# Attention, an expert layer and a tanh layer in one kernel: a rare branch made shorter, its count moved ahead, and a conversion step moved to GpSimd

## The chip, the core and the metric

One NeuronCore of a Trainium2 chip runs the whole program. The metric is the device time of one execution in microseconds, smaller is better. Before the change the median of 3 runs is 900.23 us (898.01 to 905.54). PE is TensorE, DVE VectorE, ACT ScalarE, POOL GpSimd, and SP the engine that issues most DMA transfers.

## What is computed

Three layers follow each other, all in float32, with two batches of 768 tokens.

```python
mask = q_bucket[:, :, :, None] == k_bucket[:, :, None, :]        # 6-bit sign hash of q and k
scores = np.where(mask, scale * np.matmul(q, k.transpose(0, 1, 3, 2)), -1e9)
x = softmax(scores) @ v                                          # 16 heads, then (1536, 512)
noisy = x @ w_gate + np.log1p(np.exp(x @ w_noise)) * noise       # 8 experts, the best 2 per token
out[mask] += top2_w[mask, k, None] * (np.maximum(x[mask] @ w1[e], 0) @ w2[e])
h = x @ w_in                                                     # 512 to 2048
return (h - np.tanh(h)) @ w_out                                  # 2048 to 512
```

The last layer's weights arrive as float64, and the kernel turns them into float32 itself.

## The kernel before, in words

**Precision.** A float32 product is made of three PE products: every operand is split into a high part that PE takes as it is and a low remainder, and high times high, high times low and low times high are summed. ACT makes the high part of a weight (L999), DVE or POOL the low one (L998). The same holds for activations (L1217, L1218 for inputs, L1288, L1290 for the hidden layer).

**Attention** comes first, in frames that a plan lays out; the change does not touch it.

**Experts.** Tokens are put into rows of their experts by indirect DMA. The nine segments `segs` are computed in turn: n = 0 and n = 1 are the two halves of expert 0's tokens (first batch, second batch), n = 2 to 8 the experts 1 to 7, each in eight steps f over 128 hidden columns. A step is 12 matmuls up (`h_mm`/`h_arm`, L1257) and, per block of tokens, 3 matmuls down (`y_mm`, L1297 to L1299). Segments from n = 1 on choose how many columns to multiply by the count of tokens: `ARMS` lists the widths, `pick_arm` branches on PE, `load_arm` reads the choice into a PE register. The inputs of the next segment are loaded by `load_x` and transposed by `trans_x` (L1216) during the current one.

**Segment 0 and the gate.** `seg_fine(0)` cuts segment 0 into 32 pieces (16 half steps up of 6 matmuls, 16 down products of 3 matmuls), and `fill(n, keep)` issues n of them unless only `keep` are left. They lie between the small steps of the second batch's gate (`gate(B-1)`), which DVE works off one after the other. At the end of this gate stand, in this order: the row indices for the scatter (`pick`), two low parts of weights that were held back (`lows`, L998), the totals of all experts (`totals`, L909 to L920), the arms, and the largest excess of an expert over its capacity (`excess`, L922 to L932), whose last instruction writes the count `cmi` (L931). `KEEP` pieces are left for after the branch, and `TX` says at how many remaining pieces each of segment 1's four transpositions is issued.

**The branch.** `overflow()` reads `cmi` on every engine (L1464) and enters a body only if an expert has more tokens than its 448 rows (L1465); with these inputs it is jumped over. The body is a slow, complete recomputation: a loop over experts, a loop over blocks of 128 tokens, and inside that eight hidden steps written out one after the other. Behind the branch come some warm-up products (`warm(WARM[4])`, L1649, L202), transpositions of segment 1, the kept pieces and the first step of segment 1.

**Weights and conversions.** In the loop over segments each step f may issue, on SP: `load_x`, `store()` (results of the segment before, and converted weights to the DRAM tile `W2f`, L1079), and then `fetch()` (raw weights of a coming step, L1027 to L1031). From (n, f) = (2, 3) to the end of n = 7, `convert_more` works off the float64 weights, 16 tiles of 128x1024: ACT takes the absolute value, and six DVE steps follow (L1068, L1070, L1072, L1074, L1076, L1078). The tiles `cv_g`, `cv_p`, `cv_a` and `cv_w` have one buffer each; L1076 writes `cv_w` first, L1078 adds into it, and a DMA carries it to `W2f`. Two steps are done per f, three in every odd f of n = 2 and n = 7. POOL makes low parts of weights in n = 1 and n = 7, and in n = 3 and 4 it issues nine indirect DMAs that sort an index table (`order`, L972); otherwise it has nothing to do from n = 2 to n = 6.

**Order.** PE, DVE, ACT, POOL and SP each work off their instructions in the order in which they are written, and wait for each other by semaphores.

Of the kernel before, what the change touches and what calls it, by code (L numbers as in the profile page):

```python
# [6 lines left out]
F32 = mybir.dt.float32  # L7
# [5 lines left out]
U32 = mybir.dt.uint32  # L13
# [8 lines left out]
PF = 3  # L22

FILL = (2, 0, 3, 1, 3, 1, 0, 0, 4, 2, 0, 0)
FILL2 = 2
TX = (2, 2, 0, 0)
BANKS = {'a': [0, 1, 7], 'b': [2, 3], 'c': [4, 5], 'd': [6]}

PLAN = dict(turn=(-23, -15, -19, -10), turn1=(-20, -18, -13, -10), sign=(-12, -7), sign2=5, sign1=(-9, -7), gap=0,
# [16 lines left out]

JOIN = (4, 5, 5)

WARM = (7, 1, 2, 10, 3)

POOL1 = 7

# [1 line left out]

CVN = 2

KEEP = 2

FA = 4

# [4 lines left out]

POOL_W = 4

ARMS = {0: ((96, 0), (104, 0), (112, 0), (128, 0)),
        1: ((124, 0), (128, 0), (128, 16), (128, 64))}
LN2 = 0.6931471805599453  # L70
NEGB = -8.0e9
# [17 lines left out]
def body(tc, q, k, v, proj, w_gate, w_noise, noise, w1, w2, w_in, w_out, out):  # L89
# [25 lines left out]
    with ExitStack() as ctx:  # L115
# [20 lines left out]
        def bank(tag):  # L136
            r = banks[tag]
            nbank[tag] += 1
            n = r[nbank[tag] % len(r)]
            if n in held:  # L140
                return held[n]
            return psp.tile([128, 512], F32, tag=f"b{n}", name=f"bank{n}")
# [523 lines left out]
        def gate(b):  # L666
# [120 lines left out]
            if early:  # L787
# [3 lines left out]
                eng.tensor_copy(basev[:, 1, 0:1], late0)  # L791
                eng.tensor_scalar(late0, late0, float(1 - FIRST), None, op0=ALU.add)
            yield
            ts = w("g_ts", [128, NC, E])
            if early:
                eng.tensor_scalar(ts, over, BIG, None, op0=ALU.mult)
# [123 lines left out]
            pick_arms(0, 0, 1)  # L920

        def excess():  # L922
            pick_arms(1, 1, E)
            yield
            nc.vector.tensor_tensor(exs, tots[:, 0], tots[:, 1], op=ALU.add)
            nc.vector.tensor_tensor(exs, exs, capv[:, 1], op=ALU.subtract)
            nc.vector.tensor_scalar(exs, exs, 0.0, None, op0=ALU.max)
            yield
            cmx = gx.tile([128, 1], F32, name="cmx")
            nc.vector.tensor_reduce(cmx, exs, op=ALU.max, axis=AX.X)  # L930
            nc.vector.tensor_copy(cmi, cmx)  # L931
            yield  # L932

        def results():
# [125 lines left out]
        def convert(f, t):  # L1060

            two = lambda dt: t.rearrange("p t n -> p (t n)").bitcast(dt).rearrange("p (n two) -> p n two", two=2)
            hi = two(I32)[:, :, 1]
            tl = lambda name, dt: hd["cvp"].tile([128, 2 * DM], dt, name=name)
            g, p, a, w = tl("cv_g", F32), tl("cv_p", I32), tl("cv_a", I32), tl("cv_w", F32)
            nc.scalar.activation(g, two(F32)[:, :, 1], AF.Abs)

            nc.vector.tensor_scalar(g, g, _f32(896 << 20), None, op0=ALU.max)  # L1068
            yield
            nc.vector.tensor_scalar(p, g.bitcast(I32), 3, 0x3FFFFFF8, op0=ALU.logical_shift_left, op1=ALU.bitwise_and)  # L1070
            yield
            nc.vector.scalar_tensor_tensor(a, hi, _i32(0xC0000000), p, op0=ALU.bitwise_and, op1=ALU.bitwise_or)  # L1072
            yield
            nc.vector.tensor_scalar(p, a, _i32(0xFF800000), None, op0=ALU.bitwise_and)  # L1074
            yield
            nc.vector.scalar_tensor_tensor(w, two(U32)[:, :, 0], 2.0 ** -52, p.bitcast(F32), op0=ALU.mult, op1=ALU.mult)  # L1076
            yield
            nc.vector.tensor_tensor(w, w, a.bitcast(F32), op=ALU.add)  # L1078
            stores.append(lambda: nc.sync.dma_start(out=W2f[f], in_=w))  # L1079
            yield  # L1080

# [150 lines left out]

        def pick_arm(n):
            a_, v_ = ARMS[0 if segs[n][0] == 0 else 1], AV[n]
            with tc.If(v_ > 1) as wide:  # L1235
                with tc.If(v_ > 2) as most:
                    yield a_[3]
                with most.Else():
                    yield a_[2]
            with wide.Else():  # L1240
                with tc.If(v_ > 0) as some:
                    yield a_[1]
                with some.Else():
                    yield a_[0]
# [201 lines left out]
            next(gen)  # L1446
            fill(n)
        for _ in gen:
            fill(FILL2)
        for fn_ in hd.pop("lows"):  # L1450
            fn_()
        for gen in [totals(), excess()]:
            for _ in gen:
                fill(FILL2, KEEP)
        fill(left[0], KEEP)
        load_arm(1)
        run(scatter, B - 1, 0)
# [5 lines left out]
        def overflow():  # L1463
            cnt_ = nc.values_load(cmi[0:1, 0:1], min_val=0, max_val=B * S)  # L1464
            with tc.If(cnt_ > 0):  # L1465
                run(results)
                fidx = gx.tile([128, 2, B, NC], I32, name="fidx")
                for b in range(B):
                    oh, over, t = gd[b][:3]
                    fb = gx.tile([128, E], F32, name="ub")  # L1470
                    nc.vector.scalar_tensor_tensor(fb, io8, float(YR), basev[:, b], op0=ALU.mult, op1=ALU.subtract)
                    ty = gx.tile([128, NC, E], F32, name="g_ty")
                    nc.vector.tensor_tensor(ty, t, fb[:, None, :].to_broadcast([128, NC, E]), op=ALU.add)
                    run(pick, fidx[:, :, b], oh, ty)
                nc.vector.memset(zero, 0.0)
                zero_rows(Xf, E * YR)
                for b in range(B):
                    for wh in range(2):
                        for c in range(NC):
                            nc.gpsimd.indirect_dma_start(  # L1480
                                out=Xf, out_offset=bass.IndirectOffsetOnAxis(ap=fidx[:, wh, b, c:c + 1], axis=0),
                                in_=x[:, b * NC + c], in_offset=None)
                with tc.For_i(0, E, 1) as e_:
                    with tc.For_i(0, YR, 128) as r_:
                        v_ = x[:, 0:4]
                        nc.sync.dma_start(out=v_[:, 0], in_=Xf[bass.ds(e_ * YR + r_, 128), :])
                        ps = bank("a")
                        for dc in range(KD4):
                            nc.tensor.transpose(ps[:, ck(dc)], v_[:, 0, ck(dc)], ident)
                        nc.vector.tensor_copy(v_[:, 1], ps)  # L1490
                        py = bank("d")
                        for f in range(NF):
                            r = x[:, 4:6]
                            nc.sync.dma_start(out=r[:, 0].rearrange("p (c n) -> p c n", c=KD4),
                                              in_=w1[bass.ds(e_, 1), :, f * 128:(f + 1) * 128].rearrange("o (c p) n -> p (o c) n", p=128))
                            nc.sync.dma_start(out=r[:, 1], in_=w2[bass.ds(e_, 1), f * 128:(f + 1) * 128, :].rearrange("o p n -> p (o n)"))
                            ph = bank("b")
                            for dc in range(KD4):
                                nc.tensor.matmul(ph[:, 0:128], r[:, 0, ck(dc)], v_[:, 1, ck(dc)], start=(dc == 0), stop=(dc == KD4 - 1))
                            nc.scalar.activation(v_[:, 3, 0:128], ph[:, 0:128], AF.Relu)  # L1500
                            nc.tensor.matmul(py, v_[:, 3, 0:128], r[:, 1], start=(f == 0), stop=(f == NF - 1))
                        nc.vector.tensor_copy(v_[:, 2], py)
                        nc.sync.dma_start(out=Yf[bass.ds(e_ * YR + r_, 128), :], in_=v_[:, 2])
                for b in range(B):
                    for wh in range(2):
                        for c in range(NC):
                            v_ = x[:, 0:4]
                            nc.gpsimd.indirect_dma_start(
                                out=v_[:, 0], out_offset=None, in_=Yf,
                                in_offset=bass.IndirectOffsetOnAxis(ap=fidx[:, wh, b, c:c + 1], axis=0))  # L1510
                            nc.gpsimd.indirect_dma_start(
                                out=Y, out_offset=bass.IndirectOffsetOnAxis(ap=yidx[:, wh, b, c:c + 1], axis=0),
                                in_=v_[:, 0], in_offset=None)
# [153 lines left out]
        for n in range(1, NSG):  # L1667
# [11 lines left out]
            for f in seg_steps(n, (lambda: h2_step(at(0), None)) if last else (lambda: both_step(n + 1, 0))):  # L1679
                if not last and f == fx:  # L1680
                    load_x(n + 1)
                store()
                if last and f == 4:
                    del rings["st"]
                    held_n = fn[0] - 1
                while fn[0] < min(wn[0] + (PF if "st" in rings else 2), len(wsrc)):
                    fetch()
                if not last and f == FA:
                    load_arm(n + 1)
                for dc in range(0 if last else KD4):  # L1690
# [5 lines left out]
                if n > B:  # L1696
                    next(sort, None)
                if (B, CV1) <= (n, f) < (NSG - 1, 0):
                    convert_more(CVN + (n in (B, NSG - 2) and f % 2))
                if (B, 1) <= (n, f) < (NSG - 1, 0):  # L1700
                    while conv64 and len(RAW64) + (hd.get("cv") is not None) < 2:
                        fetch64(conv64.pop(0))
                for j in range(BC if last else 0):
                    if f == j:
# [80 lines left out]
```

## Time and profile before

| | |
|---|---|
| runs | median 900.23 us, 898.01 to 905.54 |
| the profiled execution's own time | 894.86 us |
| its span | 893.1 us |
| PE busy | 865.1 us, 97% |
| DVE, ACT, POOL busy | 662.9, 537.4, 396.2 us |
| mean granted clock of TensorE | 0.994 |
| PE by fortieths of the span | 8999999999999799899999999999999999999998 |

A digit of the last line is the busy share of a slice of 22.3 us in tenths. Behind the first slice two stand out, the 7 (290 to 313 us), in which the branch lies, and the 8 (357 to 380 us), in which the conversions begin. The granted clock, 1 in most of the span, falls behind two pauses of PE, one at 263 us and one at the branch. From 600 us on the tanh layer runs, which the change does not touch either.

### The profile page before, as it was taken

The numbers are of one execution on the slowest core, as the hardware profiler recorded it, in microseconds if no ns is written. First come the engines' busy times: TensorE is split into PE (matmuls) and PEld (weight loads), VectorE is DVE, ScalarE is ACT, GpSimd is POOL, SyncE is SP. The second block draws the span as 40 slices with busy tenths as digits, with TensorE's granted clock in tenths as the row PEclk, the third lists the DMA queues.
The fourth block names the chain that finished last, engine by engine and source line by source line (L and its number), as shares of the span: only waits on it lengthen the run. The fifth ranks groups of instructions, "written<-read, shape, count | busy, mean of one in ns | idle before, by whom it ended". The sixth has DMA issues, their size and how long they took to land.

```text
span 893.1 us, 13695 instructions
## 1 busy us (share of the span) xinstructions
PE 865.1 (97%) x4625; PEld 674.1 (75%) x4625; DVE 662.9 (74%) x1275; ACT 537.4 (60%) x1027; POOL 396.2 (44%) x391
## 2 busy tenths in 40 slices
PE   8999999999999799899999999999999999999998
PEld 3555555555546599788898888788889899999996
DVE  7688778778755454878797788977987677677665
ACT  6667667766454154544344444556787677677765
POOL 6787787798894615220000005520432632632332
PEclk9999999999999899999999999999999999999999
DMA  5546645511242747896978597684300210210000
GB/s 125 136 126 199 204 139 163 161 25 39 85 161 66 247 152 217 256 309 206 294 251 299 186 326 253 216 325 136 95 25 1 76 32 1 72 36 1 24 12 36
DMA packets 111982, 127.56 MB, mean 143 GB/s; under 512 B 33744, under 2 KB 82944, under 8 KB 111888
## 3 DMA queue, kind: packets, MB, share of 16 engines
q1 hardware_dynamic: 106880, 110.81, 39.4%
q0 software_dynamic: 5008, 15.49, 5.1%
q8 instruction: 59, 0.97, 0.4%
q14 instruction: 35, 0.29, 0.1%
HBM read 82.81 MB, written 41.18 MB: 139 GB/s over the span
## 4 chain that ended last, share of the span: by engine, by line
PE 41%; DVE 7%; DMA 5%; issue 2%; ACT 2%; SPq 0%; POOL 0%; DVEq 0%; ACTq 0%; POOLq 0%
PE bank L1299 7%; PE bank L1297 7%; PE bank L1298 6%; PE bank L1257 6%; PE bank L1225 4%; PE bank L1223 4%; PE bank L1224 4%; DMA W2f<-cv_w 3%; PE bank L1264 1%; DMA wraw<-W2f 1%; DVE hh L1290 1%; DVE wt L998 1%; DVE cv_w L1076 1%; PE bank L1216 1%; DVE g_u L1586 1%
## 5 line engine op out<-in xcount | busy, mean ns | idle before, releaser
L1299 PE MATMUL bank<-wt,hh 128*128 128x512 f32 (+1 forms) x392 | 156.0, 398 | 3.3 <-DVE hh L1290 3.1
L1297 PE MATMUL bank<-wt,hh 128*128 128x512 f32 (+1 forms) x392 | 156.5, 399 | 2.1 <-PEq L1235 1.1
L1298 PE MATMUL bank<-wt,hh 128*128 128x512 f32 (+1 forms) x392 | 154.4, 394 | 0.0
L1579 POOL TENSOR_TENSOR g_th<-g_h,g_th 128x384 f32<-128x384 f32 x64 | 67.0, 1048 | 184.0 <-ACT g_th L1578 183.3
L1257 PE MATMUL bank<-xh,wt 128*128 128x400 f32 (+3 forms) x512 | 139.5, 336 | 0.1
L476 ACT ACTIVATE p<-bank 128x384 f32<-128x384 f32 x192 | 92.0, 489 | 68.6 <-PE bank L475 57.2
L441 DVE TENSOR_REDUCE mx<-bank 128x1 f32<-128x384 f32 x192 | 103.3, 551 | 36.9 <-PE bank L440 34.8
L998 POOL TENSOR_TENSOR wt<-wraw,wt 128x512 fp32r<-128x512 f32 x30 | 44.4, 1501 | 159.2 <-ACT wt L999 154.8
L999 ACT ACTIVATE wt<-wraw 128x1024 fp32r<-128x1024 f32 x75 | 79.2, 1055 | 40.1 <-PE bank L1299 17.5
L1257 PEld LDWEIGHTS bank<-xh,wt 128*128 128x128 f32 x512 | 92.9, 189 | 1.6 <-issue 0.2
L1299 PEld LDWEIGHTS bank<-wt,hh 128*128 128x128 f32 (+1 forms) x392 | 73.3, 187 | 24.9 <-DVE hh L1290 6.4
L1257 PE MATMUL bank<-xl,wt 128*128 128x400 f32 (+3 forms) x256 | 85.0, 332 | 1.9 <-DVE xl L1218 1.9
L1297 PEld LDWEIGHTS bank<-wt,hh 128*128 128x128 f32 (+1 forms) x392 | 73.5, 188 | 17.4 <-issue 3.0
L1225 PE MATMUL bank<-xh,wt 128*128 128x384 f32 x256 | 86.2, 337 | 0.0
L1223 PE MATMUL bank<-xh,wt 128*128 128x384 f32 x256 | 86.1, 336 | 0.0
L509 POOL TENSOR_TENSOR ps<-ps,p 128x768 f32<-128x768 f32 x45 | 82.3, 1829 | 8.4 <-DVE ps L509 3.3
L1224 PE MATMUL bank<-xl,wt 128*128 128x384 f32 x256 | 85.9, 336 | 0.0
L998 DVE TENSOR_TENSOR wt<-wraw,wt 128x1024 fp32r<-128x1024 f32 (+1 forms) x64 | 73.5, 1152 | 14.5 <-ACT wt L999 14.3
L500 PE MATMUL bank<-p,v 128*64 128x384 f32 x384 | 83.8, 515 | 0.0
L1298 PEld LDWEIGHTS bank<-wt,hh 128*128 128x128 f32 (+1 forms) x392 | 73.5, 187 | 13.0 <-issue 0.2
L474 PE MATMUL bank<-qc,kb 108*128 108x384 f32 (+1 forms) x192 | 79.1, 412 | 1.1 <-DVE qc L464 1.0
L1288 ACT ACTIVATE hh<-bank 128x448 fp32r<-128x448 f32 (+2 forms) x72 | 36.0, 500 | 68.3 <-PE bank L1264 20.7
(317 smaller groups left out, 1823.2 us busy)
## 6 DMA issues: line engine op xcount, KB each, us to landing
wraw<-in_moe_w_dram SPq DMA_DIRECT2D x118, 256.0 KB
cv_t<-in_moe_w_in_dram SPq DMA_DIRECT2D x16, 512.0 KB
cv_t<-in_moe_w_out_dram SPq DMA_DIRECT2D x16, 512.0 KB
W2f<-cv_w SPq DMA_DIRECT2D x16, 512.0 KB
wraw<-W2f SPq DMA_DIRECT2D x16, 512.0 KB
Xg<-zero SPq DMA_DIRECT2D x14, 512.0 KB
xy<-Xg SPq DMA_DIRECT2D x7, 768.0 KB
Y<-xy SPq DMA_DIRECT2D x7, 768.0 KB
```

Of the source, the lines that this page charges most:

```text
L441: nc.vector.tensor_reduce(MX[i % 2][:, c, hf:hf + 1], ps[:, :HF], op=ALU.max, axis=AX.X)
L476: nc.scalar.activation(hd["p", i, kc][:, half(hf)], ps[:, :HF], AF.Exp, scale=float(D) ** -0.5)
L500: nc.tensor.matmul(hd["o", i][hf * D:(hf + 1) * D, :HF], raw["v", g][:, par, kc], hd["p", i, kc][:, half(hf)], start=(kc == 0), stop=(kc = ...
L509: eng.tensor_tensor(t, hd["p", i, 0] if kc == 1 else t, hd["p", i, kc], op=ALU.add)
L998: low = lambda eng, h: eng.tensor_tensor(t[:, 1, h], r[:, h], t[:, 0, h].bitcast(F32), op=ALU.subtract)
L1223: nc.tensor.matmul(ps[:, :n], ws(0, dc), xh[:, dc, :n], start=(dc == 0), stop=False)
L1224: nc.tensor.matmul(ps[:, :n], ws(0, dc), xl[:, dc, :n], start=False, stop=False)
L1225: nc.tensor.matmul(ps[:, :n], ws(1, dc), xh[:, dc, :n], start=False, stop=(dc == KD4 - 1))
L1257: nc.tensor.matmul(col(ps), t[:, w_, 0, ck(dc)], col(x_[l_][:, dc]), start=(dc == 0 and (w_, l_) == (0, 0)), stop=(dc == KD4 - 1 and w_ == 1))
L1297: nc.tensor.matmul(ps[:m], a, t[:, 0, 1], start=first, stop=False)
L1298: nc.tensor.matmul(ps[:m], a, t[:, 1, 1], start=False, stop=False)
L1299: nc.tensor.matmul(ps[:m], l, t[:, 0, 1], start=False, stop=last)
```

## The change

Four things are edited.

1. The body of the branch: the eight hidden steps become a third loop. Its sum is kept in SBUF by DVE instead of in PSUM.
2. Around the branch: `totals()` and `excess()` move up into the gate, ahead of the scatter's indices and of the held low parts, and in `excess` the count is made before the arms of experts 1 to 7. `KEEP` goes from 2 to 8, `TX` from (2, 2, 0, 0) to (4, 4, 2, 2), the 3 warm-up matmuls go, and segment 1 has two widths to choose from (104 and 128 columns per block) instead of four (96, 104, 112, 128).
3. In the loop over segments `fetch()` comes before `store()`, and in n = 1 it may run 3 steps ahead instead of 2.
4. Conversions: L1076 writes in place, so that `cv_w` is written by the last step alone; that step is done by POOL in n = 3 to 6; the third step per f falls in f = 1 and 5 of n = 3 to 6; the first float64 weights are fetched one f sooner, and only one tile until f = 3.

```diff
-TX = (2, 2, 0, 0)
+TX = (4, 4, 2, 2)
-WARM = (7, 1, 2, 10, 3)
+WARM = (7, 1, 2, 10, 0)
-KEEP = 2
+KEEP = 8
+ADD = (3, 4, 5, 6)
-ARMS = {0: ((96, 0), (104, 0), (112, 0), (128, 0)),
+ARMS = {0: ((104, 0), (128, 0)),
@@ gate
             yield
+            if not early:
+                yield from totals()
+                yield from excess()
             ts = w("g_ts", [128, NC, E])
@@ excess
-            pick_arms(1, 1, E)
-            yield
             nc.vector.tensor_tensor(exs, tots[:, 0], tots[:, 1], op=ALU.add)
...
             nc.vector.tensor_copy(cmi, cmx)
+            yield
+            pick_arms(1, 1, E)
             yield
@@ convert
-            nc.vector.scalar_tensor_tensor(w, two(U32)[:, :, 0], 2.0 ** -52, p.bitcast(F32), op0=ALU.mult, op1=ALU.mult)
-            yield
-            nc.vector.tensor_tensor(w, w, a.bitcast(F32), op=ALU.add)
+            u = p.bitcast(F32)
+            nc.vector.scalar_tensor_tensor(u, two(U32)[:, :, 0], 2.0 ** -52, u, op0=ALU.mult, op1=ALU.mult)
+            yield
+            (nc.gpsimd if hd["n"] in ADD else nc.vector).tensor_tensor(w, u, a.bitcast(F32), op=ALU.add)
             stores.append(lambda: nc.sync.dma_start(out=W2f[f], in_=w))
@@ pick_arm
+            if len(a_) == 2:
+                with tc.If(v_ > 0) as wide:
+                    yield a_[1]
+                with wide.Else():
+                    yield a_[0]
+                return
@@ the end of the gate
         for _ in gen:
-            fill(FILL2)
+            fill(FILL2, KEEP)
         for fn_ in hd.pop("lows"):
             fn_()
-        for gen in [totals(), excess()]:
-            for _ in gen:
-                fill(FILL2, KEEP)
         fill(left[0], KEEP)
@@ overflow
-                        py = bank("d")
-                        for f in range(NF):
+                        nc.vector.memset(v_[:, 2], 0.0)
+                        with tc.For_i(0, FF, 128) as f_:
...
-                                nc.tensor.matmul(py, v_[:, 3, 0:128], r[:, 1], start=(f == 0), stop=(f == NF - 1))
-                        nc.vector.tensor_copy(v_[:, 2], py)
+                            nc.tensor.matmul(py, v_[:, 3, 0:128], r[:, 1], start=True, stop=True)
+                            nc.vector.tensor_tensor(v_[:, 2], v_[:, 2], py, op=ALU.add)
@@ the loop over segments
-                store()
...
-                while fn[0] < min(wn[0] + (PF if "st" in rings else 2), len(wsrc)):
+                while fn[0] < min(wn[0] + (PF if "st" in rings or n < B else 2), len(wsrc)):
                     fetch()
+                store()
...
-                    convert_more(CVN + (n in (B, NSG - 2) and f % 2))
-                if (B, 1) <= (n, f) < (NSG - 1, 0):
-                    while conv64 and len(RAW64) + (hd.get("cv") is not None) < 2:
+                    hd["n"] = n
+                    convert_more(CVN + (n in ADD and f % 4 == 1))
+                if (B, 0) <= (n, f) < (NSG - 1, 0):
+                    while conv64 and len(RAW64) + (hd.get("cv") is not None) < (1 if (n, f) < (B, CV1) else 2):
                         fetch64(conv64.pop(0))
```

## Rows read from the trace of the kernel before

**Rows 1.** Waits of PE: engine, tile, line, releaser: us in total, times, longest.

```profile
PE bank L1216 <- issue: 5.4, 1, 5.4
...
PE bank L1264 <- DVE hh L1290: 2.8, 2, 1.6
PE bank L516 <- DVE ps L509: 2.2, 1, 2.2
```

**Rows 2.** Timeline of PE around the branch: start us, us, line, operation, tiles, shape.

```profile
303.02 0.40 PE L1298 MATMUL bank<-wt,hh 128*96 128x512 f32 x1
303.25 0.40 PE L1299 MATMUL bank<-wt,hh 128*96 128x512 f32 x1
303.89 0.81 PE L202 MATMUL bank<-wz 128*32 128x512 bf16 x3 [0.25 <-PEq L1465]
304.63 0.55 PE L1216 MATMUL bank<-ident,xy 128*128 128x128 f32 x3
310.56 0.47 PE L1216 MATMUL bank<-ident,xy 128*128 128x128 f32 x1 [5.38 <-issue]
...
314.10 0.44 PE L1257 MATMUL bank<-xh,wt 128*128 128x192 f32 x1
```

**Rows 3.** Busy time by stretch: length, engines, then PEclk, DMA share, GB/s.

```profile
265.00:270.00 5.00, 4.70 (x24) 2.57 (x24) 0.88 (x3) 1.36 (x5) 5.00 (x4) 0.66 0.36 107
305.00:310.50 5.50, 0.18 (x2) 0.00 (x0) 0.42 (x1) 0.38 (x1) 4.05 (x5) 0.73 1.05 402
310.60:314.10 3.50, 3.50 (x11) 2.54 (x12) 0.42 (x1) 0.43 (x2) 1.74 (x2) 0.50 0.73 275
```

**Rows 4.** DMA queues, 288 to 308 us: packets, MB, share of 16 engines.

```profile
q1 hardware_dynamic: 2672, 2.08, 32.4%
q0 software_dynamic: 516, 1.71, 24.5%
q14 instruction: 2, 0.02, 0.3%
```

**Rows 5.** The same, 308 to 310 us: the queue q8.

```profile
q8 instruction: 1, 0.02, 2.9%
```

**Rows 6.** Timeline of DVE, 295 to 300.5 us.

```profile
295.11 2.36 DVE L998 TENSOR_TENSOR wt<-wraw,wt 128x1024 fp32r<-128x1024 f32 x2
297.39 0.17 DVE L916 COPY tots<-bank 128x24 f32<-128x24 f32 x1
...
300.33 0.15 DVE L931 CAST cmi<-cmx 128x1 int32<-128x1 f32 x1
```

**Rows 7.** Busy time of PE, PEld, DVE, ACT, POOL in four later stretches.

```profile
360.00:378.00 18.00, 15.30 (x78) 12.57 (x77) 16.68 (x24) 10.42 (x14) 2.98 (x3) 1.00 0.81 243
378.00:445.00 67.00, 64.14 (x320) 56.34 (x319) 53.10 (x76) 30.60 (x40) 6.04 (x4) 1.00 0.81 266
445.00:540.00 95.00, 95.00 (x485) 84.69 (x484) 79.19 (x115) 43.50 (x59) 0.00 (x0) 1.00 0.78 262
542.00:602.00 60.00, 57.33 (x284) 49.21 (x284) 51.08 (x64) 29.86 (x40) 32.33 (x22) 1.00 0.83 286
```

**Rows 8.** Waits of DVE, 320 to 606 us.

```profile
DVE cv_w L1076 <- DMA W2f<-cv_w: 15.6, 4, 5.5
```

**Rows 9.** The chain that ended last, from 425 us: start us, us, what.

```profile
429.84 10.56 DMA W2f<-cv_w
```

**Rows 10.** Two lines' instructions: count, duration ns min/median/max, first and last start.

```profile
L1078 DVE TENSOR_TENSOR cv_w<-cv_w,cv_a x16: 1207/1214/1912, 371.3 to 582.4; 128x1024 f32<-128x1024 f32 x16
...
L998 POOL TENSOR_TENSOR wt<-wraw,wt x30: 1267/1292/2316, 60.0 to 578.3; 128x512 fp32r<-128x512 f32 x30
```

**Rows 11.** Waits of POOL.

```profile
POOL PT L972 <- DMA PT<-tab,posi: 38.2, 8, 6.9
```

**Rows 12.** Groups of PE by shape: count, busy us, mean ns.

```profile
L1216 PE MATMUL bank<-ident,xy 128*128 128x128 f32 x120 | 18.5, 279 | 5.4 <-issue 5.4
L1257 PE MATMUL bank<-xh,wt 128*128 128x192 f32 x64 | 12.3, 278 | 0.1
```

More of the change, by code (lines that the diff above doesn't have):

```diff
@@ L1490, in overflow @@
                         nc.vector.tensor_copy(v_[:, 1], ps)
-                        py = bank("d")
-                        for f in range(NF):
+                        nc.vector.memset(v_[:, 2], 0.0)
+                        with tc.For_i(0, FF, 128) as f_:
                             r = x[:, 4:6]
                             nc.sync.dma_start(out=r[:, 0].rearrange("p (c n) -> p c n", c=KD4),
-                                              in_=w1[bass.ds(e_, 1), :, f * 128:(f + 1) * 128].rearrange("o (c p) n -> p (o c) n", p=128))
-                            nc.sync.dma_start(out=r[:, 1], in_=w2[bass.ds(e_, 1), f * 128:(f + 1) * 128, :].rearrange("o p n -> p (o n)"))
-                            ph = bank("b")
+                                              in_=w1[bass.ds(e_, 1), :, bass.ds(f_, 128)].rearrange("o (c p) n -> p (o c) n", p=128))
+                            nc.sync.dma_start(out=r[:, 1], in_=w2[bass.ds(e_, 1), bass.ds(f_, 128), :].rearrange("o p n -> p (o n)"))
+                            ph, py = bank("a"), bank("d")
                             for dc in range(KD4):
```

## The prediction

> **What bounds the kernel now.** The page's first part says that PE is busy for nearly the whole span, so time can be won only where PE waits or runs at the lower clock. I read the waits of PE first. The largest has no releaser: once, 5.4 us, ahead of a transposition at L1216, put down to "issue" [rows 1]; below it stands DVE. The timeline places the large one [rows 2]: PE's last product ahead of the branch starts at 303.25 us, the 3 warm-up matmuls at 303.89, three transpositions at 304.63, then nothing until 310.56, and segment 1's first product starts at 314.10. It waits for no data: the transposition after the gap is one of eight alike, of which three had run.
>
> What it lacks, the queues show. From 305 to 310.5 us the DMA share is 1.05 [rows 3]. The queue q8, which carries instructions, brings no packet from 288 to 308 us [rows 4] and one between 308 and 310 us [rows 5], just before PE goes on. I read this as PE having run out of instructions behind a jump while the next block stood behind weight loads and scatters. Behind the gap the granted clock is 0.50 [rows 3], the lower level of 1.2 GHz, so the remaining matmuls take twice their time.
>
> Then the table by stretches [rows 7]: PE loses 2.7 of 18 us where the conversions begin, 2.9 of 67 us after that, nothing from 445 to 540 us, 2.7 of 60 us at the end. DVE is busy for 93% of the first stretch, and in the second it waits for the store of the converted weights, 15.6 us in 4 waits [rows 8], one such store taking 10.56 us [rows 9]; the longest wait of PE on a late DVE is 1.6 us [rows 1].
>
> **Part 1, the branch.** From the end of the last product (303.48 us; 303.02 and 303.25 show that one takes 0.23) to 314.10 us are 10.6 us [rows 2]. The work in them is 6 matmuls of 0.23 and 8 transpositions of 0.13 (three take 0.55 us, each 0.28 long and overlapping [rows 2, 12]), 2.4 us. So 8.2 us are lost: 0.4 at the jump, 0.7 for warm-up matmuls, 5.4 in the gap with 0.2 around it, 1.5 by the lower clock.
>
> After the change 6 more pieces lie behind the jump: 12 down matmuls of 0.23 and 12 up of 0.13 (192 columns take the mean of a transposition's 128, 278 and 279 ns [rows 12]), 4.3 us. PE thus reaches the jump at 303.5 - 4.3 = 299.2 us. The count must be there by then. Now it is written at 300.48 us [rows 6], and PE's first instruction behind the jump starts 3.4 us later [rows 2]; I keep the 3.4. Ahead of the count went two low parts, 2.36 us, with the totals taken at 297.39 only after them [rows 6]; these, the indices and the arms of experts 1 to 7 go behind it, some 3.8 us of DVE's time. One of the instructions left ahead waits for a hidden step of PE, so I take 2.5 of the 3.8: count at 298.0, PE on at 301.4. PE waits 2.2 us there instead of 0.4.
>
> Behind it come the eight pieces (18 matmuls of 0.23, 12 of 0.13), 5.7 us, and 1.0 of transpositions, with no gap: the body is shorter by 7 of 8 hidden steps on PE (35 matmuls), less what a third loop adds, so the target lies nearer to what PE has loaded; and PE asks for its next block while the held low parts still keep their buffers, before the weight loads that filled the queues [rows 3]. Segment 1 then starts at 301.4 + 6.7 = 308.1 us, 6.0 us sooner. Ends: 8.2 (the whole loss goes) and 0.7 (the warm-up matmuls alone); I take 6.0, since it is summed from rows.
>
> On the other queues: DVE does the low parts (2.36 us) ahead of its own jump, and behind that makes the remainder of a hidden step which the sixth piece needs; two pieces down and two up (3.0 us) and the first transpositions cover it, and without them PE would wait about 1 us. POOL's 12 scatters start some 2 us later; `load_x` of segment 2 waits for them on SP and holds the weight loads behind it, and its transpositions come only in segment 1's sixth step, which covers both; without that cover PE would wait those 2 us. Widths: 208 columns instead of 192 in 96 matmuls cost 0, since the time does not change from 128 to 192 [rows 12]; at most 16 columns of 0.42 ns each, one per cycle at 2.4 GHz, 0.6 us.
>
> **Part 2, the conversions.** `cv_w` is now written one step later, so that a store of 10.56 us [rows 9] has three steps f instead of two, and its wait leaves DVE: of the 2.9 us that PE loses from 378 to 445 us [rows 7] I count 2.6. From 360 to 378 us DVE gets two conversion steps per f instead of two or three: of 2.7 us I count 2.2. At the end n = 7 has 16 conversion steps instead of 20: of 2.7 us 1.0, since POOL works there still and the read of `W2f` stays. Loads ahead of stores and the earlier float64 fetch: 0, PE waits for no load in these stretches, and fetches that come late are covered by the steps of lead.
>
> Twelve of the sixteen last steps (1.21 us each on DVE [rows 10]) go to POOL. POOL's nearest row is 1.29 us for half the size [rows 10], so one takes 2.6 us. It runs beside DVE, and from 542 us on, where POOL makes low parts, the same DVE instruction takes up to 1.91 instead of 1.21 us [rows 10]. Per step DVE saves 1.2 and pays between 0 and 2.6; I take 0.7 to 1.2 and count a loss on PE of 1.0 us in all. Part 2: 2.6 + 2.2 + 1.0 - 1.0 = 4.8 us, ends 0 and 7.3.
>
> By the Trainium skill, the page SBUF — State Buffer (section Who interferes with whom), a DVE instruction with two SBUF inputs and a GpSimd instruction that reads SBUF block each other fully, not in part; that would make it the 2.6 of the bounds, 12 times. The trace shows 0.7 beside it where both run, so the sum keeps its value.
>
> **Sum.** 6.0 + 4.8 = 10.8 us. The profiled execution's own time is 894.9 us, which gives 884.1. The median of the runs stands 5.4 us above it; I take the difference from the median: 900.2 - 10.8 = 889.4 us.
>
> **Rivals.**
> 1. The gap stays: a jump costs PE its next block wherever it lands. For it: the gap lies just behind the jump. Against it: PE ran three warm-up matmuls and three transpositions behind the jump, so the target was there and only what followed was missing. Part 1 then brings 0.7, the whole 5.5 us: 894.7 us. The Trainium skill has it as a rule, Runtime: NRT & Kernel Launch (Instruction fetch mechanics): a taken branch to a target outside the loaded window waits for its block; the six matmuls after the jump speak against that case here.
> 2. PE waits for the count. The 2.2 us at the jump are as long as the wait at L516 [rows 1], behind which the clock of 265 to 270 us was 0.66 [rows 3], 1.7 us of loss; part 1 then brings 4.3: 891.1 us. Against it: the count may come sooner than the 2.5 us that I took.
> 3. Part 2 brings nothing, since the steps stay on the chain of n = 3 to 6 or other waits take their place: 894.2 us. For it: PE loses nothing from 445 to 540 us, where some seven of POOL's steps are added (three per segment).
> 4. Slower: POOL's step holds up DVE. The next conversion overwrites `cv_p`, which POOL reads, so DVE waits for POOL there; and POOL's queue has index DMAs ahead of it in n = 3 and 4, each with a wait of up to 6.9 us [rows 11]. If each of the twelve makes PE late by the longest such wait, 1.6 us [rows 1], 19.2 us are lost and the 5.8 of part 2 are not won: 900.2 - 6.0 + 19.2 = 913.4 us. It decides from where DVE's free time is used up: 15.8 of 95 us from 445 to 540 [rows 7], with seven steps in them, 2.3 us each; net they cost at most 2.6 - 1.2 = 1.4, which speaks against it.
>
> **How the numbers follow.** Forecast 0.53, rivals 0.12, 0.12, 0.16 and 0.07. About 1% (9 us) is what a measurement here can tell from no change, so faster means below 891.2 us. The forecast's own range is 884.7 (both upper ends, 15.5 us) to 894 (the upper half of part 1 without part 2, or the reverse), about 0.8 of it below 891.2; with half of rival 2, a quarter of rival 3 and little of rival 1, faster has 0.53; slower has most of rival 4, 0.06; the rest, 0.41, is the same. The range of 8 in 10 takes this and rivals 1 to 3, up to 894.7, and 2.5 us at either end for the spread of the runs, a third of theirs: 882 to 897 us.
>
> **What would show it.** The 5.4 us at L1216 gone from PE's waits, a clock of 1.00 around 310 us, segment 1's first product near 308.1 us: part 1. A block on q8 that comes more than a few us after the jump, or PE waiting ahead of the jump for over 2 us: rivals 1 and 2. The wait of `cv_w` on its store gone from DVE, and PE losing under 1 us in each of the first two stretches: part 2. POOL's `cv_w` steps near 2.6 us, with DVE waiting on POOL at L1070 and PE losing time between 445 and 540 us: rival 4. The forecast is wrong if PE still pauses for over 3 us between 296 and 312 us, or if its waits on DVE from 320 to 606 us do not fall.

## The result and the profile after

The changed kernel takes 891.33 us in the median of 6 runs (888.65 to 892.47), the kernel before 900.18 us beside it (895.94 to 905.54): a ratio of 0.9896, 95% interval 0.9861 to 0.9932, about 9 us less (6 to 12.5). Run once more (e5 below) it had 0.9889 (0.9866 to 0.9912). The forecast of 889.4 us was right in sign and 1.9 us off in size; the median stands 0.1 us above the 891.2 that the prediction set for "faster". How the gain comes about differs from the forecast in several steps.

| | before | after |
|---|---|---|
| profiled execution's own time, us | 894.9 | 892.5 |
| its span, us | 893.1 | 890.7 |
| DVE busy, us | 662.9 | 655.6 |
| POOL busy, us | 396.2 | 437.0 |

The two traces are a poor pair: that of before is an execution 5.3 us below its median, that of after the slowest of its six, already late before the change begins (PE's last product of the attention starts at 276.87 us before and 279.38 us after). So I compare stretches between PE's own landmarks, not clock readings.

PE's waits after, the largest, and its only one on DVE over 1 us behind the attention:

```profile
PE bank L1222 <- DMA xy<-Xg: 6.3, 1, 6.3
PE bank L1276 <- DVE xy L1341: 2.4, 3, 2.0
```

The 5.4 us on "issue" [rows 1] are gone. In their place stands a wait for a transfer, `load_x` of segment 2. Timeline of PE after, at the branch and at that wait (as [rows 2]):

```profile
301.80 0.27 PE L1370 MATMUL bank<-xh,wt 128*128 128x192 f32 x1
302.22 0.45 PE L1309 MATMUL bank<-wt,hh 128*96 128x512 f32 x1
...
308.61 0.26 PE L1269 MATMUL bank<-xh,wt 128*128 128x208 f32 x1
...
332.69 0.66 PE L1222 MATMUL bank<-ident,xy 128*128 128x128 f32 x2 [6.26 <-DMA xy<-Xg]
```

PE runs through the jump: its branch stands at 300.9 us, while products issued earlier still run, and segment 1's first product comes at 308.61 instead of 314.10 us, though this trace is 2.5 us late. Busy time by stretch (as [rows 3, 7]; the third column from the right is the granted clock, then DMA share and GB/s):

```profile
308.60:326.40 17.80, 17.80 (x121) 15.95 (x119) 10.57 (x36) 8.57 (x14) 9.85 (x9) 1.00 0.66 226
326.40:332.70 6.30, 0.04 (x2) 0.04 (x1) 0.00 (x0) 0.00 (x0) 2.38 (x2) 0.81 0.68 223
332.70:337.00 4.30, 4.30 (x21) 4.12 (x21) 1.25 (x2) 2.03 (x3) 0.72 (x1) 0.50 1.11 344
...
360.00:378.00 18.00, 17.30 (x93) 15.16 (x93) 16.28 (x23) 10.95 (x15) 0.00 (x0) 1.00 0.78 249
378.00:445.00 67.00, 66.20 (x334) 58.91 (x333) 52.17 (x76) 30.93 (x42) 25.09 (x14) 1.00 0.80 257
445.00:540.00 95.00, 93.01 (x467) 82.73 (x466) 77.85 (x109) 43.59 (x59) 19.08 (x7) 0.98 0.82 273
542.00:602.00 60.00, 59.39 (x306) 53.08 (x305) 48.96 (x63) 31.32 (x43) 36.68 (x22) 1.00 0.81 273
```

Behind the new wait the granted clock is 0.50, the level of 1.2 GHz, as it was behind the old gap. Below, PE loses 0.7, 0.8, 2.0 and 0.6 us instead of 2.7, 2.9, 0 and 2.7 [rows 7]: the third stretch has got worse.

**Why `load_x` is late.** Timeline of POOL and SP after (POOL's scatters of x rows, SP's load):

```profile
306.93 0.98 POOL L851 DMA_INDIRECT Xg<-x,sidx  x1 [0.30 <-issue]
314.40 0.98 POOL L851 DMA_INDIRECT Xg<-x,sidx  x1 [6.49 <-DMA Xg<-x,sidx]
...
325.29 0.98 POOL L851 DMA_INDIRECT Xg<-x,sidx  x1 [0.30 <-issue]
...
328.10 0.34 SPq L1209 DMA_DIRECT2D xy<-Xg  x1
```

In the kernel before all 12 scatters stand ahead of POOL's branch. With the count made sooner, 4 do; where the branch's paths join again POOL waits until those have landed, amid the weight loads (DMA share 0.99 from 310.6 to 314.1 us), and issues the other 8 from 314.40 us. SP waits 14.0 us for them at L1209, with the weight loads behind it.

### The profile page after: what moved, and what is told of

Its sections match the earlier page's. It is cut to its first block, busy times and chain, and to the rows that moved or that the text cites. A ratio compares the mean times of both kernels' runs of the same rounds, so it can differ in the third digit from the quotient of the medians.

```text
span 890.7 us, 13686 instructions
## 1 busy us (share of the span) xinstructions
PE 866.2 (97%) x4622; PEld 677.3 (76%) x4622; DVE 655.6 (74%) x1261; ACT 536.6 (60%) x1027; POOL 437.0 (49%) x403
## 3 DMA queue, kind: packets, MB, share of 16 engines
q1 hardware_dynamic: 106880, 110.81, 39.6%
## 5 line engine op out<-in xcount | busy, mean ns | idle before, releaser
L1309 PE MATMUL bank<-wt,hh 128*128 128x512 f32 (+1 forms) x392 | 156.2, 399 | 2.4 <-PEq L1247 1.2
L1004 ACT ACTIVATE wt<-wraw 128x1024 fp32r<-128x1024 f32 x75 | 78.8, 1055 | 21.4 <-PE bank L1311 17.9
L1084 POOL TENSOR_TENSOR cv_w<-cv_p,cv_a 128x1024 f32<-128x1024 f32 x12 | 33.5, 2792 | 114.7 <-DVE cv_p L1082 46.3
L1309 PEld LDWEIGHTS bank<-wt,hh 128*128 128x128 f32 (+1 forms) x392 | 73.8, 188 | 17.5 <-issue 2.7
L511 POOL TENSOR_TENSOR ps<-ps,p 128x768 f32<-128x768 f32 x45 | 82.4, 1830 | 7.4 <-ACT p L478 2.9
L1300 ACT ACTIVATE hh<-bank 128x448 fp32r<-128x448 f32 (+2 forms) x72 | 36.2, 503 | 79.0 <-issue 25.4
L1003 DVE TENSOR_TENSOR wt<-wraw,wt 128x1024 fp32r<-128x1024 f32 (+1 forms) x64 | 75.3, 1182 | 5.2 <-ACT wt L1004 4.9
```

What stands on the lines that cost most here:

```text
L511: eng.tensor_tensor(t, hd["p", i, 0] if kc == 1 else t, hd["p", i, kc], op=ALU.add)
L1309: nc.tensor.matmul(ps[:m], a, t[:, 0, 1], start=first, stop=False)
```

## The experiments

Ratios are to runs of the kernel before on the same chip, whose median is 891.49 us for e1 to e4, 899.07 us for e5 to e8 and 898.88 us for e9 to e12. One profile each gives the stage table: us between PE's landmarks, read off the timelines. A: start of the attention's last product with v (L500 before) to segment 1's first product; B: on to the first transposition for segment 2; C: for segment 3; D: for segment 4; E: for segment 7; F: for the tanh layer.

| kernel | A | B | C | D | E | F | ratio (95%) |
|---|---|---|---|---|---|---|---|
| before | 37.2 | 18.2 | 24.7 | 43.2 | 120.1 | 82.0 | |
| e12 before | 39.6 | 17.8 | 24.6 | 40.1 | 119.6 | 82.2 | 1.003 (0.9995 to 1.006) |
| after | 29.2 | 24.1 | 26.8 | 38.4 | 123.2 | 78.6 | 0.990 (0.986 to 0.993) |
| e5 after | 29.3 | 22.1 | 25.4 | 38.4 | 122.8 | 78.6 | 0.989 (0.987 to 0.991) |
| e1 scatters first | 29.5 | 19.0 | 24.7 | 38.4 | 120.9 | 78.6 | 0.990 (0.987 to 0.993) |
| e9 scatters first | 29.4 | 24.8 | 24.7 | 38.4 | 121.3 | 78.7 | 0.987 (0.983 to 0.991) |
| e7 the same, adds on DVE | 29.4 | 25.8 | 24.7 | 38.4 | 118.9 | 78.7 | 0.986 (0.984 to 0.989) |
| e10 after, adds on DVE | 29.3 | 21.9 | 26.7 | 38.4 | 118.9 | 78.8 | 0.986 (0.982 to 0.990) |
| e2 part 1 | 29.2 | 22.8 | 27.4 | 43.1 | 123.0 | 81.0 | 1.002 (0.9996 to 1.0045) |
| e11 part 1 | 29.3 | 21.9 | 25.0 | 42.7 | 120.4 | 82.4 | 0.994 (0.991 to 0.997) |
| e8 new order alone | 29.3 | 22.2 | 25.8 | 40.3 | 120.1 | 80.7 | 0.992 (0.990 to 0.995) |
| e4 loop alone | 30.0 | 19.3 | 24.8 | 41.5 | 119.0 | 82.3 | 0.994 (0.991 to 0.996) |
| e6 loop and part 2 | 39.2 | 17.9 | 24.6 | 38.3 | 122.6 | 78.4 | 0.993 (0.991 to 0.996) |
| e3 part 2 | 35.9 | 18.2 | 24.6 | 38.3 | 123.2 | 78.6 | 0.992 (0.990 to 0.995) |

**e1, e9: the scatters ahead of POOL's branch.**

```diff
-            cnt_ = nc.values_load(cmi[0:1, 0:1], ...)
+            with tc.issue_after(scat[-1].ins):
+                cnt_ = nc.values_load(cmi[0:1, 0:1], ...)
```

> The changed kernel with one edit: GpSimd reads the count of the overflow branch only behind all 12 scatters of x rows, instead of behind 4 of them. Theory (the order on GpSimd makes the load of segment 2's rows late): the last scatter then ends near 318 us instead of 326, the load of segment 2 is issued near 322.5 us (in the kernel before it followed the last scatter by 4.6 us), lands near 327, and PE's wait of 6.3 us at L1222 falls below 1 us, with no half clock behind it; about 6 to 8 us below the changed kernel, some 16 us below the kernel before. Rival (the weight loads fill the DMA queues and the load lands late whatever GpSimd does): the wait at L1222 stays above 4 us and the time is that of the changed kernel, some 9 us below the kernel before.

882.99 us, ratio 0.9902. The wait is gone: POOL's last scatter starts at 314.51 us, the load and PE's transpositions at

```profile
319.24 0.34 SPq L1209 DMA_DIRECT2D xy<-Xg  x1
```
```profile
325.15 1.10 PE L1222 MATMUL bank<-ident,xy 128*128 128x128 f32 x8
```

with nothing idle ahead of them. So the order on POOL did cause the wait. But the time is 8.5 us below the kernel before, not the forecast 16, and the ratio no lower than that of the changed kernel. Repeated:

> The changed kernel with the 12 scatters ahead of GpSimd's branch, again, now beside the changed kernel's other variants on one chip, since its first ratio (0.990, on a chip where the kernel before takes 891 us) can't be told from that of the changed kernel (0.989 and 0.990, where it takes 899 and 900 us). Theory A (the scatters behind the join cost the changed kernel 2 to 6 us): ratio 0.983 to 0.987, no wait over 1 us at L1222. Theory B (the earlier load of segment 2 and the weight loads only push the loss to DVE and ScalarE, which then run out of instructions in segment 1, as 1.6 and 3.5 us in the profile of the variant with the additions on DVE): ratio 0.988 to 0.991, gaps of PE of over 3 us in sum between 305 and 345 us.

888.58 us, ratio 0.9873 (0.9832 to 0.9914), between the two theories. The gaps that theory B forecast are in this profile: `load_x` is in time again, but B takes 24.8 us. PE stands 1.6 and 1.8 us at L1309, with the lower clock in between, for `hh`, which ACT and then DVE make. ACT's timeline:

```profile
313.00 0.38 ACT L1300 ACTIVATE hh<-bank 128x256 fp32r<-128x256 f32 x1 [3.19 <-PE bank L1269]
319.42 0.39 ACT L1300 ACTIVATE hh<-bank 128x256 fp32r<-128x256 f32 x1 [6.04 <-PE bank L1269]
```

The products that it reads start their last matmuls at 310.22 and 311.56 us, so PE is not what it lacks. A late block of instructions, as I had expected, can't be behind the first standstill: the first on q14 [rows 4] after 305 us starts at 313.4 us, when ACT has gone on. For the second it stays possible: two more start at 317.03 and 317.38 us, 2.4 and 2.0 us before ACT goes on (2.3 and 2.2 us in e7). e7 has the same two standstills with the same lags behind the count (12.5 and 18.9 us, within 0.03), e1, the same program as e9, has none. What holds ACT there is open.

**e2, e11: part 1 alone** (the changed kernel with the conversion lines and the place of `store()` as before).

> The kernel before with part 1 alone: the loop in the overflow branch, eight pieces behind it, the count sooner, the two arms of segment 1; the conversions and the order of loads and stores as before. Theory (the gap at the branch goes and comes back at the transpositions of segment 2): segment 1's first product near 308 us instead of 314, the wait at L1222-like transpositions of segment 2 about 6 us with half clock behind it, so between 0 and 2 us are left of 8: time 0 to 2 us below the kernel before. Rival (the late load of segment 2 comes from the new order of weight loads and stores, which is not in this kernel): no such wait, time 6 to 8 us below.

> The kernel before with part 1 alone (loop, new order, two arms), again: it was 2 us above the kernel before on a chip where that takes 891 us, while the new order without the loop was 7.4 us below on one where it takes 899 us. Theory A (the loop spoils what the order wins): ratio 1.000 to 1.004 here too. Theory B (the kernel before loses more on some chips, at the branch or in the attention, and the same loss is what part 1 takes away there): on a chip with a time near 899 us for the kernel before, ratio 0.990 to 0.994, as with the order alone; on one near 891 us, 1.000 to 1.004.

893.46 us, ratio 1.002, which is 2 us above the kernel before (0.4 below to 4 above) where 0 to 2 below were forecast; on another chip 895.39 us, ratio 0.9942. In the two profiles A falls to 29.2 and 29.3 us and the transpositions wait 4.9 and 2.8 us for `load_x` without the new order of weight loads, which answers e2's rival:

```profile
PE bank L1221 <- DMA xy<-Xg: 4.9, 1, 4.9
```

That the ratio differs between the two chips (theory B of e11) was measured; what the kernel before does otherwise on the chip where it takes 891 us was not profiled.

**e3: part 2 alone.**

> The kernel before with part 2 alone: conversions written one step later, twelve last steps on GpSimd, loads ahead of stores; the branch as before. Theory (the two traces: PE loses 8.3 us from 360 to 606 us before, 4.1 after): 4 to 6 us below the kernel before, the gap of 5.4 us at the branch is there, PE loses under 1 us in each of the stretches 360 to 378 and 378 to 445 us. Rival (the whole gain of the change, 9.4 us by the medians, is this part, as part 1 gives all back): 9 us below.

885.83 us, ratio 0.9924: 5.7 us below by the medians, 6.8 by the ratio (4.3 to 9.2), nearer to its theory than to the rival's 9. The gap at the branch is there (4.4 us at L1219). From 378 to 445 us PE loses 2.3 us, though, not under 1: POOL's steps, below.

**e4: the loop alone; e6: the loop with part 2.**

```diff
-                        for f in range(NF):
+                        with tc.For_i(0, FF, 128) as f_:
```

> The kernel before with one edit: the body of the overflow branch as a loop over the eight pieces of the hidden layer instead of eight copies; the order of pieces and count as before. Theory A (the length of the skipped body decides: with a short one the code behind it is at hand): PE's gap of 5.4 us behind the jump is gone, segment 1 starts some 7 us sooner. Theory B (the moment of the jump decides: the next block of instructions stands behind weight loads whatever the length): the gap stays within 1 us, time within 1 us of the kernel before.

> The kernel before with the loop in the overflow branch and part 2, without the new order of pieces and count and without the two arms of segment 1. Theory (the loop alone removes the gap, the new order brings nothing beyond it): the gains of the two alone add up, 5.1 + 5.7 us, ratio 0.988, segment 1's first product near 306 us, no wait over 1 us at the transpositions of segment 2, all 12 scatters ahead of GpSimd's branch. Rival (the count behind the low parts makes PE wait at the jump, which the new order cures): a wait of over 2 us around 300 us and a ratio of 0.992 or more.

e4: 886.35 us, ratio 0.9935, and no gap: behind the jump PE loses 1.0 us on "issue". That looked like theory A, until e6 (893.31 us, 0.9933), with the same loop and order. Its longest wait of PE, and that of e12 (PEq is PE's own sequencer; with "remote" the profile names no releaser):

```profile
PE bank L204 <- PEq L1468: 6.8, 1, 6.8
```
```profile
PE bank L202 <- remote: 5.3, 1, 5.3
```

The first warm-up matmul behind the jump waits at once in both; in the first trace of before PE ran six matmuls further [rows 2]. A shorter body thus doesn't cure the gap dependably (the gap is in e6's trace and not in e4's), and e6's forecast that the two gains add up failed. Nor is it a wait for the count, as e6's rival has it: PE's branch, which needs the count, stands at 306.2 us (below), ahead of the 6.8 us.

**e8: the new order alone**, the body unrolled as before.

> The kernel before with the new order of pieces and count and the two arms of segment 1, but the branch's body unrolled and the conversions as before. Theory (the length of the skipped body makes the gap, not the place of the jump): PE still pauses over 3 us behind the jump, which now comes some 3 us sooner, and the load of segment 2 is late as well, as only 4 scatters stand ahead of GpSimd's branch: 1 to 6 us slower than the kernel before. Rival (an earlier jump meets free DMA queues, so the block is there in time): no pause over 1 us behind the jump, time as with the whole of part 1, 0 to 3 us above the kernel before.

891.69 us, ratio 0.9923, 7 us below the kernel before; both forecasts had it no faster. I had expected the gap to stay; it is gone with the long body too. This settles which edit of part 1 takes the gap away: the new order, which puts the jump 4 to 5 us sooner and ahead of the held low parts and of the weight loads that follow them. PE's branch, in the traces of e8 and e6:

```profile
L1473 PEldq COMPARE_BRANCH  x1: 358/358/358, 301.9 to 301.9; - x1
```
```profile
L1468 PEldq COMPARE_BRANCH  x1: 364/364/364, 306.2 to 306.2; - x1
```

The next block on q8 starts at 302.96 us in e8, 1.1 us after the branch, and at 310.64 us in e6, 4.4 us after it. So it is in every trace, and the load on the DMA queues from the jump to the block goes with it: 1.1 us at a DMA share of 0.01 to 0.07 (after, e2, e5, e8, e10, e11), 1.7 to 1.9 us at 0.5 to 0.6 (e1, e7, e9, where two blocks of 8 KB come in between as well), 3.8 to 4.8 us at 1.06 to 1.08 with the old order (e4, e12, e6, e3, before). The block itself takes 0.9 to 1.3 us. That it is the load that delays the block is read from these 14 traces; no run changed the load alone. In e4 the block is late too (3.8 us), but PE had instructions to go on with for over 4 us. One row is the changed kernel from 301 to 304 us, the other e4 from 302 to 305.3 us:

```profile
DMA packets 4, 0.02 MB, mean 8 GB/s; under 512 B 2, under 2 KB 2, under 8 KB 2
```
```profile
DMA packets 991, 1.32 MB, mean 401 GB/s; under 512 B 72, under 2 KB 674, under 8 KB 990
```

**e5: the change again; e7, e10: the twelve last steps on DVE** (e7 with the scatters first too).

```diff
-            (nc.gpsimd if hd["n"] in ADD else nc.vector).tensor_tensor(w, u, a.bitcast(F32), op=ALU.add)
+            nc.vector.tensor_tensor(w, u, a.bitcast(F32), op=ALU.add)
```

> The changed kernel as it is, on the same chip and beside the same runs of the kernel before as three variants. Against the kernel before it first had a ratio of 0.990, the variant with the 12 scatters ahead of GpSimd's branch also 0.990 on another chip, though its profile had none of the 6.3 us at L1222. Theory A (the wait at L1222 is in nearly every execution and counts in full): the profile shows 4 to 6.5 us at L1222, and the ratio lies 0.5 to 0.9 points above that of the variant with the scatters first. Theory B (the wait is covered later, or occurs only in some executions): no wait in the profile, or the same ratio within 0.3 points as the variant with the scatters first.

> The changed kernel with the 12 scatters ahead of GpSimd's branch, and the twelve last steps of the conversions on DVE instead of GpSimd, at the same places. Theory A (GpSimd's steps cost more than they give: DVE waits 5 to 9 us for them at the next conversion, and PE loses 1.1 to 2.3 us at a time by it): PE's gaps of over 1 us between 378 and 540 us are gone, DVE's waits on GpSimd too, and the time is 1 to 3 us below the same kernel with the steps on GpSimd. Theory B (DVE has no room for twelve steps of 1.2 us more): PE loses 2 us or more beyond that from 378 to 606 us, the time is 2 us or more above.

> The changed kernel with one edit: the twelve last steps of the conversions on DVE instead of GpSimd. Theory A (GpSimd's steps cost 2 to 4 us net): PE loses under 1 us from 378 to 540 us instead of 2.8 to 3.7, no waits of DVE on GpSimd in the conversions, time 2 to 3 us below the changed kernel, ratio about 0.986. Theory B (the gain of the variant with both edits came from the scatters): ratio 0.988 to 0.991 as the changed kernel.

e5: 889.53 us, with 2.4 us at L1222, below theory A's 4 to 6.5; its ratio is within 0.3 points of those of e1 and e9, as theory B has it. e7: 886.93 us, all its runs (886.68 to 887.18) below all of e5's (888.07 to 890.39) on the same chip. e10: 886.19 us beside 888.58 us of e9, ratio 0.9856; its interval overlaps that of the changed kernel, so the stages decide. E falls by some 3 us in both (the sum is under part 2 below), so theory A holds: the steps are better left on DVE. PE's two stretches in e10:

```profile
378.00:445.00 67.00, 67.00 (x340) 59.95 (x339) 58.48 (x82) 31.27 (x42) 5.56 (x4) 1.00 0.88 274
445.00:540.00 95.00, 94.72 (x481) 84.12 (x480) 83.94 (x119) 45.03 (x61) 2.22 (x2) 1.00 0.84 281
```

e7 beats both kernels on its chip. e10 beats the kernel before, and was not run beside the changed kernel; which of e7 and e10 is faster the runs don't tell.

**e12: the kernel before.**

> The kernel before as it is, for a second profile of it on the same chip as three variants. The ratio is 1.000 within its interval. Theory A (the gap at the branch is in nearly every execution): PE pauses 4 to 7 us behind the jump, the block of instructions lands 4 us or more after it, clock 0.50 behind it. Theory B (it varies between executions and chips, which makes the spread of 14 us of the kernel before): no pause of over 2 us, or one somewhere else.

900.63 us. The gap is there, 5.3 us, but ahead of the first warm-up matmul, and stage A is 2.4 us longer than in the first trace.

## Why the prediction was right, and where it was not

**Part 1: 6.0 us forecast, 2.7 found.** Stage A is 38.0 us in the mean of the four traces with the gap (before, e12, e3, e6; 35.9 to 39.6) and 29.2 to 29.5 in the nine with the new order: 8.7 us, about the upper end of 8.2 (8.0 against the trace that the prediction read). The count came when it was forecast (written by 300.45 us, less the trace's late start of 2.5 is 297.9; forecast 298.0). The wait of 2.2 us at the jump did not come: I had PE go on 3.4 us after the count, as before, but its sequencer read the count at 300.5 us while queued products still ran, and PE went on at 302.22 after a gap of 0.15 us. The 3.4 us of before were not the count's way to PE: until 303.25 us PE still had products of its own to start [rows 2]. The cause of the gap was right, and of the two reasons given for its end one holds: the block is asked for ahead of the weight loads (e8). The other, the shorter body, does not (e6). The 208 columns cost nothing: 0.26 us for the product at 308.61, 0.27 for that of 192 at 301.80.

The step that failed is the one on the other queues: "POOL's 12 scatters start some 2 us later; `load_x` of segment 2 waits for them on SP", with its price "without that cover PE would wait those 2 us". I saw that `load_x` waits for the scatters, but took them to move as one; the first did start 2.3 us later, counted from the attention's last product, but eight changed sides of POOL's branch, and the last was 13.6 us later (311.66 us before, 325.29 after), 11.1 so counted. In the six traces with 4 scatters ahead (after, e2, e5, e8, e10, e11), B is 22.5 us in the mean instead of 18.0 (before, e12, e3, e6), and C 26.2 instead of 24.7: 6.0 us given back, and 8.7 - 4.5 - 1.5 = 2.7 are left. Most of B's loss is the wait for `load_x` (6.3 us after, 4.9, 2.4, 2.7 and 2.8 in e2, e5, e10 and e11), but not all: in e8 it is 0.4 us, and PE waits 2.0 us for `hh` from ACT instead, as it does for 0.6 to 1.1 us in e5, e10 and e11. C is 26.7 to 27.4 us in the three traces with a lower clock in it (after, e2, e10; mean 0.90 to 0.94) and 25.0 to 25.8 in the others. The 2.7 are rough: A, B and C together are 78.8 to 82.0 us in the four traces and 76.1 to 80.1 in the six. That undoing it (e1, e9) gains nothing sure is the second half: in two of the three profiles with the scatters first (e9, e7) ACT stands still instead.

**Part 2: 4.8 us forecast, 4.6 found, by two errors that cancel.** D + E + F are 243.9 us in the mean of the six traces without it (before, e12, e2, e11, e8, e4), 239.3 in the six with it (after, e5, e1, e9, e3, e6), 236.0 in e7 and e10; single traces give 241.0 to 247.1, 237.9 to 240.2, and 236.0 and 236.1. So later writing and redistribution bring 7.9 us (forecast 2.6 + 2.2 + 1.0 = 5.8), and POOL's twelve steps cost 3.2 (forecast 1.0). Of the 7.9, D has 3.4 (41.8 to 38.4) and E 1.5 (120.4 to 118.9 in e7 and e10), as forecast for the first two stretches, 4.9 for 4.8, though E without part 2 is anywhere from 119.0 (e4) to 123.0 us (e2), so its 1.5 is not shown; F has 3.0 (81.8 to 78.7) where 1.0 was forecast for the end. The mis-sized terms are thus the end and POOL's steps. DVE's wait of `cv_w` on the store [rows 8] is gone with the steps on DVE too, so moving the write a step later was enough.

**Rival 4 was at work, at a sixth of its price.** The waits of DVE and POOL from 360 to 606 us, after:

```profile
DVE cv_p L1075 <- POOL cv_w L1084: 5.0, 2, 3.3
```
```profile
POOL cv_w L1084 <- DMA W2f<-cv_w: 32.8, 4, 14.9
```

The store's wait has moved to POOL, and DVE waits for POOL before it can overwrite `cv_p`. A second cost shows in the timeline at 456 us:

```profile
455.94 2.40 POOL L1084 TENSOR_TENSOR cv_w<-cv_p,cv_a 128x1024 f32<-128x1024 f32 x1 [14.89 <-DMA W2f<-cv_w]
```
```profile
456.14 2.75 DVE L1073 TENSOR_SCALAR cv_g<-cv_g 128x1024 f32<-128x1024 f32 x1 [0.40 <-ACT cv_g L1071]
...
462.54 0.67 DVE L1341 TENSOR_TENSOR xy<-bank,xy 64x512 f32<-64x512 f32 x1
```
```profile
463.36 0.72 PE L1276 MATMUL bank<-wt,hh 128*128 128x512 f32 x1 [1.99 <-DVE xy L1341]
```

DVE's instruction, 0.69 us in the median, takes 2.75: it ends 0.55 us after POOL's, blocked nearly throughout. DVE then works without a pause up to L1341, for which PE waits 2.0 us. The DVE instructions that run beside the twelve steps are together 5.1 us longer than the lower quartile of the same instructions (2.2 to 5.1 us in six traces); beside seven of the twelve they are no longer at all. The Trainium skill, SBUF — State Buffer (Who interferes with whom), says that a tensor_scalar in a mode of two ports and a GpSimd instruction shut each other out for a whole instruction; the 2.75 us agree, though the trace does not name the mode. The prediction weighed that page's rule for DVE instructions with two SBUF inputs and kept the smaller value; "fully" was right for the block, though not all twelve steps meet one. POOL's steps took 2.39 to 3.33 us (forecast 2.6).

**Rivals 1 to 3.** Rival 1 (the gap stays) did not come, but its mechanism is the one at work in e6 and e12, where PE waits at the jump itself; the change escapes it by the time of the jump. Rival 2 is out: no wait for the count, clock 1.00. Rival 3 is out by stages D and F. Neither of the signs came that would have made the forecast wrong: from 296 to 312 us PE pauses for 0.15 us at most, and its waits on DVE from 320 to 606 us fall from 7.5 to 3.3 us.

**What stays open.** The stages give 2.7 + 4.6 = 7.3 us; the medians 9 (6 to 12.5) and 10 (8 to 12). Both profiled executions of the kernel before lie below its medians (894.9 and 896.7 against 900.2 and 900.6), so its slower executions lose something more that no trace shows. That 889.4 came so near to 891.33 is thus in part luck: the stages account for 7.3 of the forecast 10.8 us.

## What to carry to other kernels

Ahead of a rare branch, look at what the DMA queues carry at the moment of the jump, since the next block of instructions goes through them: moving the jump ahead of a burst of loads took the gap away in all nine traces, shortening what is jumped over in one of two. When a branch is moved, list for every engine which instructions end up on its other side, and what its join waits for. Moving one step to an idle engine moves its waits too: here the store's wait went to POOL and came back to DVE through a single buffer.

## What was not expected of the hardware

- PE's next block of instructions, 16 KB, started 1.1 us after the jump on near-empty queues, 1.7 to 1.9 us after it at a DMA share of 0.5 to 0.6 and 3.8 to 4.8 us after it at about 1.06.
- The same program, profiled twice, went on for six matmuls behind the jump in one execution and for none in the other (before, e12).
- ACT stood still for 3.2 and 6.0 us in segment 1 with PE's products ready (e7, e9) and did not in e1.
- GpSimd's join waited 6.5 us for the landing of 4 indirect DMAs, with the DMA share at 0.99.
